# A decode step of two layers on one core: another order of the work around the two token mixers between the layers

## The chip, the cores and the metric

The kernel runs on one core of one Trainium2 chip; the other cores are idle. The time is that of one execution on the device, in microseconds (us). Three runs of the kernel before took 2510.24, 2511.62 and 2512.16 us, the median is 2511.62.

## The reference

Two layers, each an attention block and a token mixer with residuals, for B = 2 sequences with one new token each (D = 512):

```python
x = x + A(layernorm(x), k_cache, v_cache, wq, wo)   # 32 query heads, 8 K/V heads, 32768 keys, head width 128
x = x + M(layernorm(x), w1, b1, w2, b2)             # for each of the D channels: 1 token -> 1792 hidden, gelu -> 1 token
x = x + A(...)                                      # the same caches and weights again
x = x + M(...)
```

`A` is softmax attention (`q = x @ wq`, four query heads share one K/V head, scores times 128^-0.5), followed by `@ wo`. All numbers are float32. Both layers read the same caches: 2 x 8 heads x 32768 keys x 128 numbers, once for K and once for V, 537 MB in all. They don't fit on the chip, so almost all of it is read from HBM twice.

## The kernel before, in words

**Units and chunks.** A unit is one K/V head of one sequence in one layer; there are 32, numbered `n` in the order of `units`. Its K and its V are cut into 8 chunks of 4096 keys (2 MB each). `load_k` and `load_v` issue the loads, all from SyncE's (SP's) queue through `load` (L136). `k_chunk` (L413) multiplies a K chunk with the unit's query columns into a PSUM tile `scores`, one tile for chunks 0 to 3 and one for 4 to 7 (the two halves of a unit); behind the last chunk of each half a maximum is taken on VectorE (L423). `max_1` (L429 to L433) and `max_2` (L437, L439) make one maximum per head of it, `turn_scores` (L443) transposes the scores into the SBUF tiles `S[0]` and `S[1]`, and the exponential is taken by `exponentials` (L448) or, for the units 14 and 17, by `exponentials_at_once` (L460 on VectorE, L463 on ScalarE) with `sums` (L467) for the denominators. `v_chunk` (L553) multiplies the V chunks with `S` into the PSUM tile `acc`. `out_0` (L521, L523), `out_1` (L593, L595) and `out_2` (L236) bring the unit's result through `wo` into the PSUM tile `rows`.

**Memory.** The tile `mem` holds cells of 2 MB (one chunk; 16 KB per partition). Loads go to whole cells, to pairs of cells or to half cells. `spread` picks for a chunk in the middle part of the kernel: a whole cell if one is free early enough (`fit` of at least 2), otherwise two halves, each with its own load of 1 MB. A load waits until what stood in its cell has been read.

**Residents.** Of head 7 (the "keeper") the K chunks 0, 1 and 2 (cells 0, 1 and 9) and parts of V stay in the chip's memory from layer 0 to layer 1. So unit 15 (layer 1, sequence 0, head 7) starts with three K chunks that need no load, and so does unit 18 for sequence 1. Once they are read, their cells take other chunks.

**The changes of layer.** After unit N1 = 13 sequence 0 is done with the attention of layer 0, after N2 = 16 sequence 1. Then comes its mixer, while K of the next unit, which still belongs to layer 0 or to the other sequence (14, and 17), streams through. The mixer's steps: `mix_1` (L615) puts x, broadcast over the partitions, into a PSUM tile `bcast`; `take_rows` (L607, L608) copies `rows` to `S[1]`; `mix_2` adds them to `bcast` (L639) and takes mean and deviation of the layer norm (L642 to L647, one power on GpSimd, L628); `hidden_sum` makes 14 tiles, each a gelu on ScalarE (L778) and a multiply-add into `acc` on VectorE (L793, L795); `mix_3` adds the sum over partitions to `bcast` (L803), copies it out (L805) and takes the statistics of the new x (L811 to L814); `to_columns` (L302, L305, L307) turns the row into the columns of x and of its layer norm. Only then can the query of unit 15 or 18 be made (`make_q`: L338 products, L347, L351, L359).

**What sets the order.** The order is written by hand (`manual_schedule`): each engine's instructions stand in the order in which the program issues them. The main loop walks over `stream`, a list of K and V chunks sorted by a key; chunk number `t` of it is time `t`. `at(time, f, ...)` hangs a function behind that time; with half steps it stands between the two halves of a chunk. Functions of one time run by rank. The allocator (`fit`, `hold`, `booked`, `closed`) reckons in the same times. `vend` is the time at which unit n's last V chunk is done, `kend` that of its last K chunk; in a change K chunks 2 to 7 of the next unit stand at `vend` to `vend + 6`.

The order around the first change, on TensorE: V chunk 7 of unit 13; K2, first half; `out_1`; K2, second half; `out_2`; K3, first half; `mix_2`; K3, second half; K4, K5; K6, first half; `mix_3`; K6, second half; `to_columns`; K7, first half; the query products of unit 15; K7, second half; the query columns; `max_1`; resident K0 of unit 15 with `max_2` in the middle; then V and resident K in turn: V0, K1, V1, K2, V2, K3 and so on. K2 and K3 of unit 14 are loaded as whole cells, K4 to K7 and V0 to V2 as halves.

Of the kernel before, what the change touches and what calls it, by code (L numbers as in the profile page):

```python
# [13 lines left out]
P = 128  # L14
# [28 lines left out]
def gqa_mixer_kernel(ctx: ExitStack, tc: tile.TileContext, x, kt, v, wqo, cols, out):  # L43
# [118 lines left out]

    def spread(until):

        k = min((*range(WCELL0 + 1), KEPT[3][1]), key=lambda k: (-fit(k, 1, until), idle(k)))
        if fit(k, 1, until) >= 2:
            hold(k, 1, until)
            return [cells(k)]
        return [half(until - 0.5), half(until)]
# [141 lines left out]
    def unit_of(n):  # L311

        return units[n]
# [4 lines left out]
    def partner(n):  # L318

        layer, b, h = unit_of(n)  # L320
        return units.index((layer, B - 1, h)) if b == 0 and (layer == 0 or h in passing) else None

    def make_q(n, step, place=None):

# [4 lines left out]
        if n in q_kept:  # L329
            if step == 3:  # L330
                nc.vector.tensor_copy(qpad[n % 2][:, 28 : 28 + R], q_kept.pop(n))
            return
        if step == 0:

            q_ps[n] = pfix.tile([P, 512], F32, name="bcast") if N1 < n <= N3 + 2 else kept[0]
        if step < 2:
            for d in range(step * DT // 2, (step + 1) * DT // 2):
                nc.tensor.matmul(  # L338
                    q_ps[n][:m, :],
                    xnT[:, d, b : b + m],  # L340
                    wq_at(h)[:, d, :],
                    start=(d == 0),
                    stop=(d == DT - 1),
                )
        if step == 2:
# [34 lines left out]
    def load_k(n, c, m, limit):  # L380
# [4 lines left out]
        if own is not None:  # L385
            if stay and not layer:
                until = k_done[units.index((1, b, h)), c + m - 1]
            hold(own, m, until)
            bufs = [cells(own, m)]
        elif limit == RING:  # L390
            bufs = spread(until)
        else:
            bufs = [buffer(m, limit, until)]
# [9 lines left out]
    def k_chunk(n, c, part):  # L403
# [16 lines left out]
        if i == PACK - 1 and part == SUB - 1:  # L420
            if half == 0:
                mx[n] = field(n, 0, HALVES)
            nc.vector.tensor_reduce(mx[n][:, half : half + 1], sc_ps[n, half], axis=AX.X, op=ALU.max)  # L423

# [420 lines left out]
    for n in range(NU):  # L845
        stream += [(n * NCH + c + m - 1, 0, n, c, m, limit) for c, m, limit in parts(n, 0)]
        for c, m, limit in parts(n, 1):
            if n in (N1, N2):
                key = (n + 1) * NCH + 1 + (c + 1) / (2 * NCH)
            elif n in (N1 + 1, N2 + 1):  # L850
                key = (n + 1) * NCH - 0.5 + max(c / (2 * NCH) - 0.5, c + 1)
            else:
                key = (n + 1) * NCH + c + m - 1 + (LAG if N1 < n <= N3 else 0)
# [21 lines left out]
    for n in range(NU):  # L875
# [4 lines left out]
        if n:  # L880
            if n in (N1 + 2, N2 + 2):
                q0 = q1 = q2 = mixed[layer - 1, b] + 0.5
                q3 = q2 + 0.5
                place = S[1]
# [4 lines left out]
            assert q3 <= kbeg[n]  # L889
            at(q0, make_q, n, 0)  # L890
            at(q1, make_q, n, 1)
            at(q2, make_q, n, 2, place)
# [5 lines left out]
        if n in (N1 + 1, N2 + 1):  # L898
            t0 = mixed[units[n - 1][:2]]
            at(t0, turn_scores, n, 0, rank=2)  # L900
            at(kend, max_1, n)
            at(kend + 0.5, max_2, n)
            at(kend + 0.5, exponentials_at_once, n, 0)
            t1 = kend + 1
            assert t0 + 1 <= kend == kbeg[n + 1]
            at(t1, turn_scores, n, 1, rank=2)
# [29 lines left out]
        if units[n] == lay[layer, b][-1]:  # L936
            key = (layer, b)
            at(vend - 1 if change else vend, mix_1, key)
            at(vend + (1 if change else 2), take_rows, key, row_tile())
            at(vend + (1.5 if change else 3), mix_2, key)  # L940
            at(vend + (0 if change else 1), gelu_table)
            if change:

                assert k_done[n + 1, NCH - 1] == vend + 6
                at(vend + 2, hidden_sum, key, rank=2)
                at(vend + 4.5, mix_3, key)
                at(vend + 5, to_columns, key)
                mixed[key] = vend + 5
            else:
# [105 lines left out]
```

## Time and profile before

| | us |
|---|---|
| median of three runs | 2511.62 |
| the profiled execution, its own time | 2510.26 |
| its span (first to last instruction) | 2508.5 |
| TensorE matmuls, busy | 1386.6 (55%) |
| TensorE weight loads, busy | 372.2 (15%) |
| VectorE, busy | 239.9 (10%) |
| ScalarE, busy | 188.0 (7%) |
| HBM, read | 1063.81 MB, 424 GB/s over the span |
| loads of the caches and weights, share of 16 DMA engines | 98.8% |

The busy digits of the page cut the span into 40 slices of 62.7 us. The mean granted clock of TensorE is 0.767. In the rows of groups the columns are: line, engine, operation, output and inputs, count, then busy us, mean ns of one, and the idle time before them with what ended it. A matmul of the program is two on the engine here (float32), so eight records make the four matmuls of one half chunk.

### The profile page before, as it was taken

The numbers are of one execution on the slowest core, as the hardware profiler recorded it, in microseconds if no ns is written. First come the engines' busy times: TensorE is split into PE (matmuls) and PEld (weight loads), VectorE is DVE, ScalarE is ACT, GpSimd is POOL, SyncE is SP. The second block draws the span as 40 slices with busy tenths as digits, with TensorE's granted clock in tenths as the row PEclk, the third lists the DMA queues.
The fourth block names the chain that finished last, engine by engine and source line by source line (L and its number), as shares of the span: only waits on it lengthen the run. The fifth ranks groups of instructions, "written<-read, shape, count | busy, mean of one in ns | idle before, by whom it ended". The sixth has DMA issues, their size and how long they took to land.

```text
span 2508.5 us, 20487 instructions
## 1 busy us (share of the span) xinstructions
PE 1386.6 (55%) x9270; PEld 372.2 (15%) x9270; DVE 239.9 (10%) x632; ACT 188.0 (7%) x554; POOL 4.9 (0%) x17
## 2 busy tenths in 40 slices
PE   4555554645445554666577676355546555455556
PEld 1111111111111111111121121111111111111112
DVE  0000000000000000004013110000000000010002
ACT  0000000000000000002012010000000000012002
POOL 0000000000000000000000000000000000000000
PEclk8777777777777777888797887777777777777778
DMA  9999999999999999999999999999999999999996
GB/s 419 433 433 433 434 434 431 432 429 434 432 433 432 433 429 432 430 426 381 426 426 404 395 428 433 433 433 432 430 432 431 432 429 430 434 432 435 433 431 285
DMA packets 33504, 1065.14 MB, mean 425 GB/s; under 512 B 3973, under 2 KB 3977, under 8 KB 4874
## 3 DMA queue, kind: packets, MB, share of 16 engines
q1 hardware_dynamic: 33128, 1063.80, 98.8%
q8 instruction: 73, 1.20, 0.2%
q14 instruction: 13, 0.11, 0.0%
q10 hardware_dynamic: 290, 0.04, 0.0%
HBM read 1063.81 MB, written 0.00 MB: 424 GB/s over the span
## 4 chain that ended last, share of the span: by engine, by line
DMA 73%; PE 24%; DVE 1%; issue 1%; ACT 0%; SPq 0%; POOL 0%; DVEq 0%; ACTq 0%
DMA mem<-in_v_dram 37%; DMA mem<-in_kt_dram 36%; PE scores L413 11%; PE acc L553 10%; PE kept L338 1%; DVE acc L795 1%; PE rows L236 0%; PE bcast L338 0%; PE small L437 0%; PE small L593 0%; PE bcast L803 0%; PE small L584 0%; PE kept L735 0%; PE small L351 0%; PE small L302 0%
## 5 line engine op out<-in xcount | busy, mean ns | idle before, releaser
L413 PE MATMUL scores<-mem,small_sb 128*32 128x512 f32 x4096 | 635.3, 737 | 612.5 <-DMA mem<-in_kt_dram 612.4
L553 PE MATMUL acc<-mem,S 128*16 128x512 f32 x4088 | 614.1, 740 | 456.6 <-DMA mem<-in_v_dram 455.1
L413 PEld LDWEIGHTS scores<-mem,small_sb 128*32 128x32 f32 x4096 | 149.0, 128 | 997.6 <-issue 892.0
L448 ACT ACTIVATE S<-S,small_sb 128x128 f32<-128x128 f32 x240 | 123.6, 519 | 2112.4 <-DVE small_sb L439 1640.2
L553 PEld LDWEIGHTS acc<-mem,S 128*16 128x16 f32 x4088 | 134.1, 111 | 832.7 <-issue 687.9
L423 DVE TENSOR_REDUCE small_sb<-scores 128x1 f32<-128x512 f32 x64 | 44.2, 691 | 914.6 <-PE scores L413 914.6
L443 DVE STREAM_TRANSPOSE S<-scores 128x512 f32<-128x512 f32 x64 | 45.5, 710 | 129.9 <-PE acc L553 129.9
L338 PE MATMUL kept<-mem,small_sb 128*2 128x512 f32 x104 | 51.0, 616 | 1.7 <-DVE small_sb L264 1.7
L236 PE MATMUL rows<-mem,small_sb 128*1 128x512 f32 (+1 forms) x276 | 47.7, 604 | 2.6 <-ACT mem L778 2.4
L448 ACT ACTIVATION_READ_ACCUMULATOR S<-S,small_sb 128x1 f32 x240 | 44.9, 187 | 0.0
L433 DVE TENSOR_REDUCE small_sb<-small 1x4 f32<-1x128 f32 x32 | 8.9, 279 | 278.0 <-PE small L431 278.0
L523 DVE SCALAR_TENSOR_TENSOR S<-acc,small_sb,S 128x128 f32<-128x128 f32 x93 | 32.6, 351 | 3.3
L595 DVE TENSOR_TENSOR small_sb<-small,small_sb 128x4 f32<-128x4 f32 x31 | 5.1, 164 | 290.8 <-PE small L593 290.8
L586 DVE RECIPROCAL small_sb<-small 128x4 f32<-128x4 f32 x32 | 5.9, 184 | 280.6 <-PE small L584 280.6
L778 ACT ACTIVATE S<-bcast,small_sb 128x512 f32<-128x512 f32 x28 | 21.5, 777 | 98.9 <-DVE small_sb L647 96.8
L351 PE MATMUL small<-small_sb,mem 2*128 2x2 f32 x112 | 15.1, 253 | 17.9 <-DVE mem L347 17.9
L521 DVE TENSOR_SCALAR S<-acc,small_sb 128x128 f32<-128x128 f32 x31 | 10.8, 349 | 112.6 <-PE acc L553 112.6
L338 PE MATMUL bcast<-mem,small_sb 128*1 128x512 f32 (+1 forms) x40 | 19.4, 617 | 0.0
L593 PEld LDWEIGHTS small<-small_sb,S 128*128 128x128 f32 x62 | 12.4, 249 | 44.9 <-issue 40.6
L351 PEld LDWEIGHTS small<-small_sb,mem 2*128 2x128 f32 x112 | 14.0, 191 | 30.5 <-DVE mem L347 27.3
L795 DVE SCALAR_TENSOR_TENSOR acc<-S,small_sb,acc 128x512 f32<-128x512 f32 x24 | 18.1, 755 | 2.5
L431 PE MATMUL small<-small_sb 128*1 128x128 f32 x64 | 16.1, 343 | 0.6 <-DVE small_sb L429 0.6
(134 smaller groups left out, 268.1 us busy)
## 6 DMA issues: line engine op xcount, KB each, us to landing
mem<-in_kt_dram SPq DMA_DIRECT2D x35, 2048.0 KB, 20.7
mem<-in_v_dram SPq DMA_DIRECT2D x26, 2048.0 KB, 21.7
mem<-in_v_dram SPq DMA_DIRECT2D x9, 4096.0 KB, 30.0
mem<-in_wqo_dram SPq DMA_DIRECT2D x14, 2048.0 KB, 33.7
mem<-in_kt_dram SPq DMA_DIRECT2D x7, 4096.0 KB, 27.4
mem<-in_kt_dram SPq DMA_DIRECT2D x18, 1024.0 KB, 9.2
mem<-in_v_dram SPq DMA_DIRECT2D x17, 1024.0 KB, 10.4
mem<-in_v_dram SPq DMA_DIRECT2D x2, 1280.0 KB, 27.2
```

Source lines behind the costliest of these rows:

```text
L236: nc.tensor.matmul(rows[32 * g : 32 * g + b + 1, :], weights if b else weights[:, 1:], row, start=False, stop=True, skip_group_check=True,)
L338: nc.tensor.matmul(q_ps[n][:m, :], xnT[:, d, b : b + m], wq_at(h)[:, d, :], start=(d == 0), stop=(d == DT - 1),)
L351: nc.tensor.matmul(pt[:, r * m : (r + 1) * m], q_row[n][:m, r * DH : (r + 1) * DH], ident[:m, :m], start=True, stop=True,)
L413: nc.tensor.matmul(sc_ps[n, half][32 * g : 32 * g + 32, :], q, kc[k * NG + g], start=(i == 0 and k == 0), stop=(i == PACK - 1 and k == SUB ...
L423: nc.vector.tensor_reduce(mx[n][:, half : half + 1], sc_ps[n, half], axis=AX.X, op=ALU.max)
L431: nc.tensor.matmul(pm[:1, :P], mxa, ident, start=True, stop=True)
L443: nc.vector.transpose(S[half], sc_ps[n, half])
L448: nc.scalar.activation(s[:, :, h], s[:, :, h], AF.Exp, bias=neg[n][:, h : h + 1], scale=SCALE, accum_out=lsum[n][:, half, h : h + 1],)
L523: nc.vector.scalar_tensor_tensor(t, acc[:, k * DH : (k + 1) * DH], mask[:, k : k + 1], t, op0=ALU.mult, op1=ALU.add)
L553: nc.tensor.matmul(acc[32 * g : 32 * g + R * QT, :], S[half][:, col : col + R * QT], vc[q], start=(c == 0 and q < NG), stop=(c == NCH - 1 ...
L778: nc.scalar.activation(hid[key, f], px[key], AF.Gelu_apprx_tanh, bias=shift[key][:, f : f + 1], scale=slope[key][:, f : f + 1],)
L795: nc.vector.scalar_tensor_tensor(h if f == FT - 1 else acc, h, w, acc, op0=ALU.mult, op1=ALU.add)
```

## The change

Around each of the two changes of layer, and nowhere else:

- `mix_2` stands right behind `out_2` and `take_rows`, ahead of K3, and `hidden_sum` right behind it, ahead of K3's instructions instead of behind them.
- `mix_3` stands behind the second half of K6 instead of between its halves, `to_columns` and `turn_scores` of the first half between the halves of K7.
- The maximum of the first half of unit 14 (and 17) is taken behind K6's first half, so behind `hidden_sum` on VectorE.
- The query products of unit 15 (and 18) stand behind K7 and are cut up: one ahead of `max_1`, one ahead of `max_2`, two behind the exponential of the first half. The columns of the query follow V0.
- V0 and V1 of unit 14 (and 17) stand ahead of the resident K0, and each later V chunk of that unit two K chunks earlier than before, so that the order is V0, V1, K0, V2, K1, V3, K2, V4, K3 and so on; at its end K6 and K7 of unit 15 (and 18) follow each other with no V between. The second half's scores are turned behind V1.
- K2 and K3 of unit 14 (and 17) are loaded as halves. What follows from that and from the new order: V3 and V4 of unit 14 are loaded as halves too, and V2 and V3 of unit 17. There are 8 loads more in all, of the same bytes.

```diff
-    def spread(until):
+    def spread(until, parted=False):
...
-        if fit(k, 1, until) >= 2:
+        if fit(k, 1, until) >= 2 and not parted:
...
+    def q_products(n, *ds):
+
+        layer, b, h = unit_of(n)
+        m = 1 if partner(n) is None else B
+        for d in ds:
+            if d == 0:
+                q_ps[n] = pfix.tile([P, 512], F32, name="bcast") if N1 < n <= N3 + 2 else kept[0]
+            nc.tensor.matmul(
+                q_ps[n][:m, :],
+                xnT[:, d, b : b + m],
+                wq_at(h)[:, d, :],
+                start=(d == 0),
+                stop=(d == DT - 1),
+            )
...
         if step < 2:
-            for d in range(step * DT // 2, (step + 1) * DT // 2):
...
+            q_products(n, 2 * step, 2 * step + 1)
...
-            bufs = spread(until)
+            bufs = spread(until, n in (N1 + 1, N2 + 1) and c > 1)
...
-            nc.vector.tensor_reduce(mx[n][:, half : half + 1], sc_ps[n, half], axis=AX.X, op=ALU.max)
+            if half or n not in (N1 + 1, N2 + 1):
+                highest(n, half)
+
+    def highest(n, half):
+
+        nc.vector.tensor_reduce(mx[n][:, half : half + 1], sc_ps[n, half], axis=AX.X, op=ALU.max)
...
             elif n in (N1 + 1, N2 + 1):
-                key = (n + 1) * NCH - 0.5 + max(c / (2 * NCH) - 0.5, c + 1)
+                key = (n + 1) * NCH - 0.5 + max(c / (2 * NCH) - 0.5, c - 1)
...
             if n in (N1 + 2, N2 + 2):
-                q0 = q1 = q2 = mixed[layer - 1, b] + 0.5
-                q3 = q2 + 0.5
+                q2 = mixed[layer - 1, b]
+                q3 = q2 + 1
...
-            at(q0, make_q, n, 0)
-            at(q1, make_q, n, 1)
+            if n not in (N1 + 2, N2 + 2):
+                at(q0, make_q, n, 0)
+                at(q1, make_q, n, 1)
...
         if n in (N1 + 1, N2 + 1):
-            t0 = mixed[units[n - 1][:2]]
-            at(t0, turn_scores, n, 0, rank=2)
+            at(kend - 0.5, turn_scores, n, 0, rank=2)
+            at(kend, q_products, n + 1, 0)
             at(kend, max_1, n)
-            at(kend + 0.5, max_2, n)
-            at(kend + 0.5, exponentials_at_once, n, 0)
-            t1 = kend + 1
-            assert t0 + 1 <= kend == kbeg[n + 1]
+            at(kend, q_products, n + 1, 1)
+            at(kend, max_2, n)
+            at(kend, exponentials_at_once, n, 0)
+            at(kend, q_products, n + 1, 2, 3)
+            t1 = kend + 2
+            assert mixed[units[n - 1][:2]] == kend == kbeg[n + 1] - 2
...
-            at(vend + (1.5 if change else 3), mix_2, key)
+            at(vend + (1 if change else 3), mix_2, key)
...
-                at(vend + 2, hidden_sum, key, rank=2)
-                at(vend + 4.5, mix_3, key)
-                at(vend + 5, to_columns, key)
-                mixed[key] = vend + 5
+                at(vend + 1, hidden_sum, key)
+                at(vend + 4.5, highest, n + 1, 0)
+                at(vend + 5, mix_3, key)
+                at(vend + 5.5, to_columns, key)
+                mixed[key] = vend + 6
```

More of the change, by code (lines that the diff above doesn't have):

```diff
@@ L332, in make_q @@
             return
-        if step == 0:
-            q_ps[n] = pfix.tile([P, 512], F32, name="bcast") if N1 < n <= N3 + 2 else kept[0]
         if step < 2:
-            for d in range(step * DT // 2, (step + 1) * DT // 2):
[L338 to L344, printed above, removed]
+            q_products(n, 2 * step, 2 * step + 1)
         if step == 2:
```

## The prediction, made before the changed kernel ran

> **What bounds the kernel now.** I read the page first: busy tenths by slice, then the chain that ended last.
>
> ```profile
> span 2508.5 us, 20487 instructions
> DMA  9999999999999999999999999999999999999996
> GB/s 419 433 433 433 434 434 431 432 429 434 432 433 432 433 429 432 430 426 381 426 426 404 395 428 433 433 433 432 430 432 431 432 429 430 434 432 435 433 431 285
> DMA 73%; PE 24%; DVE 1%; issue 1%; ACT 0%; SPq 0%; POOL 0%; DVEq 0%; ACTq 0%
> ```
>
> The transfers are the bound: the DMA row is 9 almost to the end and they fill 73% of the chain. But the GB/s row sags in the slices with 381, 404 and 395, and there lie the two places that the change touches: the token mixer of batch 0 (after unit 13) and that of batch 1 (after unit 16), both of layer 0. I cut both out with the view by windows; its last two columns are the DMA share and GB/s.
>
> ```profile
> 1150.00:1174.00 24.00, 14.57 (x84) 2.48 (x76) 14.77 (x25) 12.86 (x17) 0.54 (x1) 0.80 1.00 407
> 1174.00:1194.00 20.00, 19.03 (x146) 6.36 (x142) 7.94 (x18) 1.26 (x2) 0.54 (x1) 0.99 0.86 306
> 1194.00:1214.00 20.00, 10.16 (x64) 2.05 (x64) 1.46 (x3) 0.00 (x0) 0.00 (x0) 0.83 1.01 430
> 1340.00:1370.00 30.00, 19.59 (x110) 3.65 (x102) 16.28 (x29) 12.85 (x17) 0.54 (x1) 0.76 1.00 420
> 1370.00:1386.00 16.00, 15.03 (x84) 5.48 (x84) 6.99 (x17) 1.26 (x2) 0.54 (x1) 0.82 0.60 212
> 1386.00:1406.00 20.00, 15.34 (x114) 4.33 (x106) 2.83 (x7) 0.00 (x0) 0.00 (x0) 1.00 1.01 431
> ```
>
> Against the 430 of the undisturbed rows, 20 us at 306 lose 20 x (1 - 306/430) = 5.77 us and 16 us at 212 lose 8.11: 13.88 us in which the DMA engines had nothing to do. The rows at 407 and 420 lose 1.28 and 0.70 more. Since the rest of the span is a stream at full rate, every us of this that goes is a us off the end.
>
> **Why it runs dry.** In a mixer the loads have five half cells of 1 MB (K chunks 2.5, 7, 7.5, 8, 8.5 in turn). A half is reloaded when TensorE has read it, so a wait on TensorE becomes a late load. First mixer, timeline (start, us, engine, line; in brackets the idle time before and what ended it):
>
> ```profile
> 1143.42 3.38 PE L553 MATMUL acc<-mem,S 128*16 128x512 f32 x16 [1.90 <-DMA mem<-in_v_dram]
> 1147.23 1.12 DVE L523 SCALAR_TENSOR_TENSOR S<-acc,small_sb,S 128x128 f32<-128x128 f32 x3
> 1148.31 1.07 PE L413 MATMUL scores<-mem,small_sb 128*32 128x512 f32 x8 [1.51 <-DMA mem<-in_kt_dram]
> 1149.31 0.39 PE L593 MATMUL small<-small_sb,S 128*128 128x4 f32 x2
> 1151.61 0.69 DVE L607 COPY S<-rows 128x512 f32<-128x512 f32 x1 [1.72 <-PE rows L236]
> 1153.21 1.06 PE L413 MATMUL scores<-mem,small_sb 128*32 128x512 f32 x8 [1.66 <-DMA mem<-in_kt_dram]
> 1154.20 1.12 PE L639 MATMUL bcast<-S,small_sb 128*128 128x512 f32 x2
> 1157.75 1.45 ACT L778 ACTIVATE S<-bcast,small_sb 128x512 f32<-128x512 f32 x2 [49.99 <-DVE small_sb L647]
> 1158.16 1.06 PE L413 MATMUL scores<-mem,small_sb 128*32 128x512 f32 x8 [0.98 <-DMA mem<-in_kt_dram]
> 1165.64 1.06 PE L413 MATMUL scores<-mem,small_sb 128*32 128x512 f32 x8 [0.94 <-DMA mem<-in_kt_dram]
> 1169.72 0.75 DVE L795 SCALAR_TENSOR_TENSOR S<-S,small_sb,acc 128x512 f32<-128x512 f32 x1
> 1170.53 2.08 PE L803 MATMUL bcast<-S,small_sb 128*128 128x512 f32 x2 [3.82 <-DVE S L795]
> 1176.27 3.17 PE L338 MATMUL bcast<-mem,small_sb 128*1 128x512 f32 x7
> 1180.81 0.69 DVE L423 TENSOR_REDUCE small_sb<-scores 128x1 f32<-128x512 f32 x1 [0.23 <-PE scores L413]
> 1185.20 1.91 PE L553 MATMUL acc<-mem,S 128*16 128x512 f32 x16 [0.65 <-ACT S L463]
> ```
>
> K chunk 6a (the first half) is read at 1165.64. TensorE then stands before L803 until the hidden sum ends at 1170.47, and afterwards has the query products (L338) and the maxima before the first V chunk, 1185.20. The loads behind these waits, from the timeline of SP and from the DMA issues of those windows (last column: us to landing):
>
> ```profile
> 1174.53 0.33 SPq L136 DMA_DIRECT2D mem<-in_v_dram  x1
> 1180.80 0.33 SPq L136 DMA_DIRECT2D mem<-in_v_dram  x1
> 1186.32 0.33 SPq L136 DMA_DIRECT2D mem<-in_v_dram  x1
> 1383.26 0.33 SPq L136 DMA_DIRECT2D mem<-in_v_dram  x1
> ```
>
> ```profile
> mem<-in_kt_dram SPq DMA_DIRECT2D x7, 1024.0 KB, 9.5
> mem<-in_v_dram SPq DMA_DIRECT2D x4, 1024.0 KB, 6.9
> mem<-in_v_dram SPq DMA_DIRECT2D x2, 1024.0 KB, 5.8
> ```
>
> The first is 1149 to 1165, the second 1174 to 1187, the third 1370 to 1384. A half takes 1.05 MB / 430 = 2.4 us to move, so a load must be issued 6.9 - 2.4 = 4.5 us (second mixer 3.4) before the queue runs dry. V1a (1174.53) just held; V2a (1180.80) and V2b (1186.32) came too late, and so did V2 of the second mixer (1383.26, a whole cell).
>
> **Part 1: halves for K2 and K3, statistics right behind the output rows.** Half of K2 lands 2.4 us ahead of the whole, at 1145.9, so K2a runs when V7 ends (1143.42 + 3.38 = 1146.8); L593 then waits only for DVE (1147.23 + 1.12 = 1148.35) and starts at 1148.4, 0.9 us earlier than 1149.31. The copy of the rows ends at 1151.61 + 0.69 - 0.9 = 1151.4, and L639, no longer behind K3a, starts there and not at 1154.20: 2.8 us earlier. So does all that hangs on it: gelus from 1154.95, hidden sum done at 1167.7. K3a waits 1.1 us behind L639, with its load's room not needed for 7 us: nothing. Second mixer:
>
> ```profile
> 1344.40 1.30 PE L413 MATMUL scores<-mem,small_sb 128*32 128x512 f32 x8 [2.99 <-DMA mem<-in_kt_dram]
> 1350.30 1.12 PE L639 MATMUL bcast<-S,small_sb 128*128 128x512 f32 x2
> 1361.73 1.93 PE L413 MATMUL scores<-mem,small_sb 128*32 128x512 f32 x8 [0.55 <-DMA mem<-in_kt_dram]
> 1365.82 0.75 DVE L795 SCALAR_TENSOR_TENSOR S<-S,small_sb,acc 128x512 f32<-128x512 f32 x1
> 1366.62 2.08 PE L803 MATMUL bcast<-S,small_sb 128*128 128x512 f32 x2 [2.96 <-DVE S L795]
> 1383.85 1.91 PE L553 MATMUL acc<-mem,S 128*16 128x512 f32 x16 [0.65 <-ACT S L463]
> ```
>
> There K2a moves from 1344.40 to 1341.9. From the start of L593 to the end of the copy it took 3.0 us in the first mixer; from the landing of K2b (1344.4) that gives 1347.4 for L639 instead of 1350.30: sum done at 1363.7 instead of 1365.82 + 0.75 = 1366.57.
>
> **Part 2: the sum (L803) behind K6b.** With a queue that never empties halves land every 2.48 us (1165.64 - 1158.16 over the three halves between these two reads, each released by a DMA). So K6b lands at 1168.1, after the sum is ready (1167.7). TensorE waits for data alone: K6b ends at 1169.2, L803 at 1170.3 (1.12 us as L639) to 1171.3 (2.08 as now), K7a (landed 1170.6), the columns, K7b (1173.0) ends at 1174.1 to 1175.2. Its loads follow: V1a at 1169.3 (now 1174.5), V2a at about 1174.7 (now 1180.80). All have over 7 us of queue ahead. The maximum of the first half (0.69 us of DVE) moves behind the sum into the 2.8 us in which DVE waits for L803: nothing, and 0.7 us ahead of V0 if that wait were gone. POOL has only the two powers of the statistics, which move with them.
>
> **Part 3: queries in the wait for maxima, V0 and V1 ahead of the resident K0.** Seven of the eight passes of the four products take 3.17 us, so one product 0.9. In the kernel before they stand ahead of K7b's maximum; now one stands before each of the two small matmuls of the maxima and two beside the exponential. From the maximum to V0 it took 1185.20 - 1180.81 = 4.4 us; with up to 0.6 more for products in front I take 4.7 to 5.5 from K7b's end: V0 at 1178.9 to 1180.7. V0a frees the room of V2b, issued at 1180.0 to 1181.8. The queue then holds V0b, V1a, V1b, V2a and ends at 1185.4: lead 3.6 to 5.4 against the 4.5 needed, a loss of 0 to 0.9, taken as 0.3. In the second mixer the same steps give V2b at 1376.2 to 1378.0 against a queue end of 1361.73 + 8 x 2.48 = 1381.5: also 0.3 at most. Behind it V3a, V3b, V4a, V4b follow TensorE with leads of 6 us and more (V0b 1181.3, then 1.1 us of query columns, V1, then K0 1.9 us, V2a 1186.3). On SP the load into K0's room now stands behind four halves of V; it is issued at 1188 with 7 us in the queue: nothing. Resident K0 no longer covers V0's wait; the price of that is rival 4.
>
> **Part 4: more halves.** In each mixer four chunks of 2 MB more are loaded as halves (K2, K3 and V3, V4; second V2, V3): 16.8 MB at 420 GB/s (window 1340:1370, almost all halves) instead of 430 costs 0.93 us, and 6.3 MB that now run in the dry stretches 0.35. The Trainium skill, "DMA: Bandwidth & Descriptors", section "Bandwidth", speaks against such a cut: it measured 341 GB/s for 1 MB against 425 for 16 MB. That is one transfer by itself, and the row of 420 disagrees for halves in a full queue; by the page the 16.8 MB would cost 10.2 us, and the whole come to some 2508 (an estimate).
>
> **Sum.** 13.88 - 0.6 - 1.28 = 12.0 us. The profiled execution took 2510.26 (span 2508.5), so 2498.3; the three runs' median is 1.4 higher, so 2499.6 against it. I say **2499.0**.
>
> **Rivals.** (1) The chain from the hidden sum, not the data, still sets V0: it now takes 1185.20 - 1170.47 = 14.7 and 1383.85 - 1366.57 = 17.3 us. Kept whole, V0 comes at 1182.4 and 1381.0, V2b 1.1 later, and 2.6 and 4.0 us stay lost: 13.88 - 6.6 - 1.3 = 6.0, **2504.3**. Against it: in these chains lie K6b, K7b and all query products, which now stand elsewhere. (2) TensorE runs at the lower clock through V and resident K, which alternate there: K 3.6 us a chunk instead of 1.9.
>
> ```profile
> 1198.22 2.74 PE L413 MATMUL scores<-mem,small_sb 128*32 128x512 f32 x12 [3.80 <-DMA mem<-in_kt_dram]
> ```
>
> That is 12 of 16 matmuls, so 3.6 the chunk. V0 then ends at 1182.8, V1 with the query columns at 1187.4, K0 at 1191.0, V2a at 1192.8. V4b, issued then, has a queue to 1185.4 + 4 x 2.48 = 1195.3, a lead of 2.5 against 4.5: 2 us in each mixer, 12.0 - 4.0 = 8.0, **2502.3**. Against it: 0.99 granted in 1174:1194, where TensorE is busy throughout. "TensorE: Matmul & The Clock Gate" of the Trainium skill, section "Part 1", has the lower clock after some 3.4 us idle; the trace agrees for L803 (3.82 idle, 2.08 us), and the wait before V0 is near that. (3) Halves fall to the 306 GB/s of the dry row: the extra 16.8 MB cost 54.9 - 39.1 = 15.8 us, 13.88 - 0.6 - 0.35 - 15.8 = -2.9, **2513**. Against it: 420. The rule of the Trainium skill in part 4 points this way. (4) Slower: TensorE's queue is in order, so V0's wait for the exponential now holds all resident chunks too, whose rooms used to come free beside it. From a wait of 11.5 us after K7b (V2b at 1186.7, 1186.7 + 4.5 - 1185.4 = 5.8 lost) the first mixer gains nothing, and each us more costs one. If the 14.7 of rival 1 stood behind K7b, 9.0 and 8.0 would be lost, 3.1 more than now, and with 1.3 for the halves it is **2515**. Against it: 4.4 measured.
>
> **Chances.** Forecast 0.68, rivals 0.13, 0.09, 0.04, 0.06. The range goes from 2495 (all of 13.88 and most of the 2 us of the 407 and 420 rows gone) to 2505, which takes in rivals 1 and 2. Faster by over 0.2% (5 us, about what a measurement of this kernel can tell from no change): 0.68 + 0.13 + 0.09 = 0.90, within 0.04, slower 0.06.
>
> **What would show it.** In the new profile slices 19 to 23 of the GB/s row should read about 420 to 430. L639 should start right behind the copy of the rows; L803 should no longer be released by DVE but follow K6b; V0 should start some 5 us after K7b's maximum; V2b should be issued before its queue ends. Wrong would be: a DMA share below 0.9 in the 20 us behind K7b, or a rate under 410 with a full queue.

## The result and the profile after

The changed kernel takes **2499.86 us** (median of 6 runs, 2499.0 to 2501.82); the kernel before, run beside it on the same chip, 2510.14 us (6 runs, 2507.17 to 2512.16). The ratio is 0.9961, 95% interval 0.9948 to 0.9974: some 10 us faster. The forecast was 2499.0 in a range of 2495 to 2505. The profiled execution took 2499.0 us with a span of 2497.2, so 11.3 us of span went. From the page of the kernel after, GB/s by slice and chain:

```profile
GB/s 420 435 435 425 437 432 433 432 431 434 435 433 430 431 432 433 428 426 411 427 426 421 428 420 427 435 434 433 429 431 436 433 429 432 436 431 432 431 431 288
DMA 74%; PE 25%; issue 0%; DVE 0%; ACT 0%; SPq 0%; POOL 0%; DVEq 0%
```

The transfers are still the bound. The slices that read 381, 404 and 395 now read 411, 421 and 428. The same six stretches in the view by windows (last three columns: granted TensorE clock, DMA share, GB/s):

```profile
1150.00:1174.00 24.00, 15.98 (x100) 3.37 (x93) 16.10 (x29) 12.86 (x17) 1.09 (x2) 0.85 1.01 409
1174.00:1194.00 20.00, 17.61 (x110) 4.93 (x106) 6.67 (x14) 1.26 (x2) 0.00 (x0) 0.84 0.99 403
1194.00:1214.00 20.00, 11.39 (x84) 2.11 (x76) 1.36 (x3) 0.00 (x0) 0.00 (x0) 0.91 1.01 430
1340.00:1370.00 30.00, 21.62 (x120) 4.63 (x120) 18.21 (x34) 13.15 (x18) 1.08 (x2) 0.89 1.01 421
1370.00:1386.00 16.00, 12.97 (x109) 3.71 (x108) 4.57 (x8) 0.97 (x2) 0.00 (x0) 1.00 1.02 424
1386.00:1406.00 20.00, 14.40 (x99) 3.89 (x94) 2.15 (x4) 0.00 (x0) 0.00 (x0) 0.91 1.01 428
```

The two dry windows went from 306 to 403 and from 212 to 424. Against 430 they now lose 20 x (1 - 403/430) = 1.26 and 16 x (1 - 424/430) = 0.22 us, where they lost 5.77 and 8.11: 12.4 us won. By the same reckoning 1.35 us are given back far away, at 1460 to 1480 (last section). The first mixer's timeline:

```profile
1147.25 0.39 PE L603 MATMUL small<-small_sb,S 128*128 128x4 f32 x2
1148.57 1.06 PE L418 MATMUL scores<-mem,small_sb 128*32 128x512 f32 x8 [0.93 <-DMA mem<-in_kt_dram]
1150.56 0.69 DVE L617 COPY S<-rows 128x512 f32<-128x512 f32 x1 [2.72 <-PE rows L236]
1151.31 1.12 PE L649 MATMUL bcast<-S,small_sb 128*128 128x512 f32 x2 [0.81 <-DVE S L617]
1154.85 1.45 ACT L788 ACTIVATE S<-bcast,small_sb 128x512 f32<-128x512 f32 x2 [47.77 <-DVE small_sb L657]
1158.50 1.07 PE L418 MATMUL scores<-mem,small_sb 128*32 128x512 f32 x8 [1.34 <-DMA mem<-in_kt_dram]
1160.97 1.94 PE L418 MATMUL scores<-mem,small_sb 128*32 128x512 f32 x8 [1.41 <-DMA mem<-in_kt_dram]
1166.82 0.75 DVE L805 SCALAR_TENSOR_TENSOR S<-S,small_sb,acc 128x512 f32<-128x512 f32 x1
1168.43 1.07 PE L418 MATMUL scores<-mem,small_sb 128*32 128x512 f32 x8 [0.95 <-DMA mem<-in_kt_dram]
1169.43 1.12 PE L813 MATMUL bcast<-S,small_sb 128*128 128x512 f32 x2
1180.03 1.91 PE L563 MATMUL acc<-mem,S 128*16 128x512 f32 x16
1181.14 3.14 SPq L136 DMA_DIRECT2D mem<-in_v_dram  x3
1189.73 1.05 PE L563 MATMUL acc<-mem,S 128*16 128x512 f32 x8 [2.39 <-DMA mem<-in_v_dram]
```

The lines have moved by ten: L649 is the product of the statistics, L805 the last step of the hidden sum, L813 the sum over partitions, L563 the V products. L813 has no bracket: it follows K6b at once, for 1.12 us where L803 took 2.08. The last two rows are V2b's load (the first of the three in its row, issued at 1181.14) and the product that waits for it. The second mixer:

```profile
1361.80 1.12 PE L813 MATMUL bcast<-S,small_sb 128*128 128x512 f32 x2
1370.39 1.91 PE L563 MATMUL acc<-mem,S 128*16 128x512 f32 x16
```

### The profile page after: what moved, and what is told of

The parts are those of the page before. It is cut to its first block, busy times and chain, and to the rows that moved or that the text cites. A ratio compares the mean times of both kernels' runs of the same rounds, so it can differ in the third digit from the quotient of the medians.

```text
span 2497.2 us, 20499 instructions
## 1 busy us (share of the span) xinstructions
PE 1385.6 (55%) x9270; PEld 371.4 (15%) x9270; DVE 240.3 (10%) x632; ACT 187.8 (8%) x554; POOL 4.9 (0%) x17
## 4 chain that ended last, share of the span: by engine, by line
DMA 74%; PE 25%; issue 0%; DVE 0%; ACT 0%; SPq 0%; POOL 0%; DVEq 0%
DMA mem<-in_v_dram 38%; DMA mem<-in_kt_dram 37%; PE scores L418 11%; PE acc L563 10%; PE kept L330 1%; PE bcast L330 1%; PE rows L236 0%; PE small L447 0%; PE small L603 0%; PE small L594 0%; PE kept L745 0%; PE small L441 0%; SPq L136 0%; ACT S L458 0%; PE small L356 0%
## 5 line engine op out<-in xcount | busy, mean ns | idle before, releaser
L563 PE MATMUL acc<-mem,S 128*16 128x512 f32 x4088 | 618.4, 743 | 462.1 <-DMA mem<-in_v_dram 457.2
L563 PEld LDWEIGHTS acc<-mem,S 128*16 128x16 f32 x4088 | 135.3, 111 | 833.1 <-issue 683.4
L236 PE MATMUL rows<-mem,small_sb 128*1 128x512 f32 (+1 forms) x276 | 49.8, 635 | 2.6 <-ACT mem L788 2.3
L805 DVE SCALAR_TENSOR_TENSOR acc<-S,small_sb,acc 128x512 f32<-128x512 f32 x24 | 18.1, 754 | 2.5
L603 PEld LDWEIGHTS small<-small_sb,S 128*128 128x128 f32 x62 | 11.5, 232 | 45.0 <-issue 37.9
L441 PE MATMUL small<-small_sb 128*1 128x128 f32 x64 | 17.3, 365 | 0.2 <-DVE small_sb L439 0.2
## 6 DMA issues: line engine op xcount, KB each, us to landing
mem<-in_kt_dram SPq DMA_DIRECT2D x26, 1024.0 KB, 11.3
```

Source lines behind the costliest of these rows:

```text
L236: nc.tensor.matmul(rows[32 * g : 32 * g + b + 1, :], weights if b else weights[:, 1:], row, start=False, stop=True, skip_group_check=True,)
L441: nc.tensor.matmul(pm[:1, :P], mxa, ident, start=True, stop=True)
L563: nc.tensor.matmul(acc[32 * g : 32 * g + R * QT, :], S[half][:, col : col + R * QT], vc[q], start=(c == 0 and q < NG), stop=(c == NCH - 1 ...
L805: nc.vector.scalar_tensor_tensor(h if f == FT - 1 else acc, h, w, acc, op0=ALU.mult, op1=ALU.add)
```

## Experiments

The theory on trial, the **lead theory**: the queue runs dry because V0, and with it the loads that wait for its room, is late; the reordering brings V0 forward, by its earlier start and by its order in about equal parts. Its rivals are named in each expectation. Below, "V0 at +x / +y" is the start of the first V product, counted from the second record of the product of `out_1` (L593, in the changed kernel L603), first / second mixer: before +35.8 / +38.0, changed kernel +32.7 / +31.4. The product of `out_1` itself moves (first mixer: 1149.31 before, 1147.25 changed), so where that matters the start in the first mixer is given too: 1185.20 before, 1180.03 changed. Rows and windows are those of one profiled execution, which can lie some us off the median. Each median stands beside those of the kernel before from the same call: 2509.4 for the first four runs, 2510.3 for the next four, 2511.3 for the three of the clock, 2510.8 for the last.

### The early start alone

The kernel before with K2 and K3 in halves and the statistics and hidden sum behind the output rows; the sum, the queries and V as before.

```diff
+            bufs = spread(until, n in (N1 + 1, N2 + 1) and c > 1)
...
+            at(vend + (1 if change else 3), mix_2, key)
...
+                at(vend + 1, hidden_sum, key)
```

> The kernel before with the earlier start of the mixer alone (K2 and K3 in halves, statistics right behind the output rows); sum, query products and the order of V and resident K stay. Lead theory (time is lost only where the load into V2b's room is issued less than 4.5 to 6 us before the queue of loads ends): first gelu 2.8 us earlier in both mixers, V0 at about 1182.4 and 1381, about half of the gain: 2504 to 2506 us. Rival (the earlier start is the whole gain): 2500 us.

**2500.2 us** (2499.48 to 2501.22; ratio 0.9963, 0.995 to 0.9976): the rival's number, the whole measured gain. Its second mixer on TensorE:

```profile
1359.34 1.48 PE L413 MATMUL scores<-mem,small_sb 128*32 128x512 f32 x8 [0.56 <-DMA mem<-in_kt_dram]
1360.99 1.12 PE L803 MATMUL bcast<-S,small_sb 128*128 128x512 f32 x2 [0.17 <-DVE S L795]
1363.05 1.05 PE L302 MATMUL small<-small_sb,S 128*128 128x1 f32 x8
1365.19 3.17 PE L338 MATMUL bcast<-mem,small_sb 128*1 128x512 f32 x7
1374.13 1.91 PE L553 MATMUL acc<-mem,S 128*16 128x512 f32 x16 [0.65 <-ACT S L463]
```

The kernel before has these in the same place, in the same order. Here are K5b, which lies well ahead of its L803 (2.08 us), and behind L803 K6b, the columns and, behind K7a, the products:

```profile
1359.24 1.93 PE L413 MATMUL scores<-mem,small_sb 128*32 128x512 f32 x8 [1.43 <-DMA mem<-in_kt_dram]
1368.62 1.94 PE L413 MATMUL scores<-mem,small_sb 128*32 128x512 f32 x8
1370.49 1.87 PE L302 MATMUL small<-small_sb,S 128*128 128x1 f32 x8
1374.00 4.08 PE L338 MATMUL bcast<-mem,small_sb 128*1 128x512 f32 x7
```

The columns (L302) take 1.05 us here in place of 1.87, the query products (L338) 3.17 in place of 4.08. From the hidden sum's end to V0 it is 13.2 us in place of 17.3. TensorE stood 0.17 us ahead of L803 in place of 2.96. So the chain of the second mixer got shorter with its order untouched, and a new theory arose, the **clock theory**: it is not the wait for the sum that costs most but the low clock that TensorE has behind it. In the kernel before the low clock did not begin with that wait: K5b already took 1.93 us, and the granted clock of the whole stretch from 1359 to 1374 is 0.50. The wait at most kept it low.

In the first mixer the start did less: V0 at 1183.73 is 1.5 us earlier than before, L803 took 2.08 us here too, behind a wait of only 1.35, and the window reads 354 GB/s in place of 306. In the second mixer it reads 410 in place of 212.

### Parts of the order alone, or taken back

V0 and V1 ahead of the resident K0 in the kernel before, nothing else:

```diff
+                key = (n + 1) * NCH - 0.5 + max(c / (2 * NCH) - 0.5, c - 1)
...
+            at(kend, max_2, n)
+            at(kend, exponentials_at_once, n, 0)
+            t1 = kend + 2
```

> The kernel before with V0 and V1 ahead of the resident K0 alone. Lead theory: V0 still waits for a hidden sum that ends at 1170.5 and for the query products ahead of K7b, so it starts at about 1184.5 instead of 1185.2 and V2b's load at about 1185.6: 0 to 2 us gained, 2508 to 2510 us. Rival (the order of V and resident K is the gain): 2500 to 2503 us.

2509.57 us (2504.69 to 2513.32; 0.9991 to 1.001): no difference. In the first mixer V0 stayed where it was (1185.10, +35.1), with 320 GB/s in the window. In the second it came at +35.0, 3.0 us earlier, with 310 GB/s in place of 212; but that profiled execution took 2506.69, and the median of the ten shows nothing of it.

The changed kernel with K0 ahead of V0 again:

```diff
-                key = (n + 1) * NCH - 0.5 + max(c / (2 * NCH) - 0.5, c - 1)
+                key = (n + 1) * NCH - 0.5 + max(c / (2 * NCH) - 0.5, c + 1)
...
-                q3 = q2 + 1
+                q3 = q2
```

> The changed kernel with the resident K0 ahead of V0 again, as before. K0 needs the query's columns, which now come behind the exponential, so V0 should start 5 us later than in the changed kernel, V2b's load at about 1186 and 1376.5. Lead theory: 5 to 6 us more lost in the first mixer, 2 to 5 in the second: 2507 to 2510 us. Rival (the earlier start is the whole gain): 2500 us.

2502.15 us (0.9966 to 0.9985), between the two expectations: V0 at +37.0 / +35.4 (1184.34 in the first mixer). So a V0 that starts 4.3 and 4.0 us later than in the changed kernel cost 2.3 us here, far less than the lead theory had.

The changed kernel with all four query products ahead of K7b:

```diff
-            at(kend, q_products, n + 1, 0)
...
-            at(kend, q_products, n + 1, 1)
...
-            at(kend, q_products, n + 1, 2, 3)
+            at(kend - 0.5, q_products, n + 1, 0, 1, 2, 3, rank=3)
```

> The changed kernel with all four query products ahead of the second half of K7, as before. Lead theory: the second half of K7 comes 3 to 3.6 us later, V0 about 2.5 us later; 2.5 us more lost in the first mixer, 0 to 2 in the second: 2502 to 2505 us. Rivals: the place of the products costs nothing, 2500 us; or all of the wait returns, 2507 us.

2504.24 us (0.9973 to 0.9992), the time that the lead theory had: V0 at +32.9 / +36.2. In the first mixer `out_1` came late too, so the +32.9 hides that V0 started at 1182.03, 2.0 us later than in the changed kernel; in the second it was 4.8 later, more than forecast. With the sum behind K6b the products ahead of K7b are in the way.

The changed kernel with the products behind V0's first half and the query columns behind V1:

```diff
-            at(kend, q_products, n + 1, 0)
...
-            at(kend, q_products, n + 1, 1)
...
-            at(kend, q_products, n + 1, 2, 3)
+            at(kend + 0.5, q_products, n + 1, 0, 1, 2, 3)
```

> The changed kernel with all four query products between the halves of V0 and the query's columns behind V1. Lead theory: V0 starts 0.8 to 1 us earlier, V2b's load with it, the first mixer loses up to 1 us less, the second nothing less (its lead of 6.0 us was enough): 2498.5 to 2500 us. Rival (resident K0, which then waits for the query behind V1, delays V2): 2 to 4 us lost, 2502 to 2504 us.

2500.7 us (0.9948 to 0.9977), not told apart from the changed kernel, though V0 in the first mixer started at 1178.22, 1.8 us earlier (+29.8 / +31.0; `out_1` came 1.0 later). A V0 earlier than the changed kernel's bought nothing measurable. By itself this run could hide a gain, because K0 now waits for columns behind V1; the last run below, which leaves them in place, says the same.

The changed kernel with K2 and K3 whole:

```diff
-            bufs = spread(until, n in (N1 + 1, N2 + 1) and c > 1)
+            bufs = spread(until)
```

> The changed kernel with K2 and K3 as whole cells again (4 loads fewer). Lead theory: the mixer starts 0.9 us later in the first and about 2.5 us later in the second change, but its sum still ends about when K6b lands, so V0 hardly moves; 0 to 0.5 us less for fewer halves: 2499 to 2500.5 us. Rival (every us of the earlier start counts): 3.4 us lost, 2503 us.

2498.72 us (0.9939 to 0.9972), the fastest median but not to be told from 2499.86: once the rest stands, these halves bring nothing and cost at most about 1 us. The run shows more than that. In its first mixer the statistics start no earlier than in the kernel before (L649 at 1154.14, there L639 at 1154.20), and the hidden sum ends at 1170.42, there at 1170.47. Yet V0 starts at 1179.89, 5.3 us earlier:

```profile
1170.47 2.07 PE L813 MATMUL bcast<-S,small_sb 128*128 128x512 f32 x2
1179.89 1.91 PE L563 MATMUL acc<-mem,S 128*16 128x512 f32 x16
```

From the sum's end to V0 it is 9.5 us in place of 14.7, with L813 at the low clock as before. Nor is there an early start in the second mixer: L649 comes 6.8 us after K2 has landed, L639 before 5.9. So the new order brings the whole gain without the early start, just as the early start brought it without the new order.

### V0 later by a known amount

Copies of `S[0]` onto itself on ScalarE ahead of the exponential of units 14 and 17, 7 and 13 of them; nothing is left out.

```diff
+        for _ in range(7 if half == 0 else 0):
+            nc.scalar.activation(S[half], S[half], AF.Copy)
         nc.scalar.activation(S[half], S[half], AF.Exp)
```

> The changed kernel with seven copies of the first half's scores onto themselves (ScalarE) ahead of its exponential in the units 14 and 17, about 4.3 us in front of V0. Lead theory: V2b's lead falls from 4.6 to about 0.3 in the first mixer (4 us more lost) and from 6.0 to 1.7 in the second (1.7 to 4.3 lost): 2505.5 to 2508.5 us. Rivals: no slack at all, 2508.6 us; a delay of V0 hidden by the queue, 2500 us.

> The same with thirteen copies, about 8 us in front of V0, so some 12.5 to 13 us from the second half of K7 to V0: the point from which the slower rival of the prediction decides (11.5 us). Lead theory: 8 us more lost in the first mixer, 5.4 to 8 in the second: 2513 to 2516 us, slower than the kernel before (2510). Rival (hidden by the queue): 2500 us.

2507.31 us (0.9978 to 0.9997) and **2513.59 us** (1.0006 to 1.0025, slower than before). V0 came at +36.7 / +36.0 and +40.0 / +40.0: 4.1 and 4.6, then 7.4 and 8.6 us later than in the changed kernel. The medians rose by 7.5 and 13.7 us for 8.7 and 15.9 us of delay, 0.86 us a microsecond. The two windows of the 13 copies (the dry stretch reaches beyond the second, with 351 GB/s in 1386 to 1406):

```profile
1174.00:1194.00 20.00, 11.41 (x68) 3.10 (x64) 5.50 (x11) 9.44 (x15) 0.00 (x0) 0.83 0.64 259
1370.00:1386.00 16.00, 7.00 (x36) 2.24 (x36) 4.67 (x12) 8.81 (x14) 0.54 (x1) 0.85 0.78 324
```

So in this order a late V0 is dear, as both theories have it. But the price is not that of V0's start alone: with K0 ahead of V0 (above) V0 stood as late as with the seven copies, 1184.34 against 1184.43 in the first mixer, and that cost 2.3 us, not 7.5. The copies hold back all that stands behind V0 on TensorE, the resident chunks too: the next load of K is issued at 1186.63 there and at 1195.99 with the seven copies. That is the mechanism of the fourth rival; that it makes the whole difference of the two runs is argued, not shown.

### The clock alone

The kernel before with nothing moved; products of the 128x128 unit matrix with itself (`idle_products`, which the kernel already has for its last mixer) keep TensorE busy while the hidden sum runs. Nobody uses them.

```diff
+                at(vend + 3, idle_products, 4, rank=3)
+                at(vend + 3.5, idle_products, 4, rank=3)
+                at(vend + 4, idle_products, 4, rank=3)
+                at(vend + 4.5, idle_products, 8, rank=0)
                 at(vend + 4.5, mix_3, key)
```

> The kernel before with nothing moved; in the two changes' mixers four products of the 128x128 unit matrix with itself (0.29 us each at the full clock, by the eight passes in 1.16 us that line 615 takes) behind each of three K halves during the hidden sum, and eight of them (2.3 us, and twice that at the low clock) in TensorE's queue right ahead of the sum of the mixer. They leave nothing out and compute nothing that is used. What they do is keep TensorE from idling 3.82 and 2.96 us ahead of the sum. Clock theory (the start-only run gained at the second mixer because TensorE no longer idled ahead of the sum): the sum's product takes 1.1 in place of 2.08 us, and the time from the hidden sum's end to V0 falls from 14.7 and 17.3 us to 13 to 14 us, so V0 comes 1 and 3.5 us earlier, at a microsecond each: 2504.5 to 2507. Rival (that chain is set by VectorE, ScalarE and the loads, or the start alone made the difference): 2509.5 to 2511.

**2503.15 us** (2500.99 to 2505.13; 0.9972, 0.996 to 0.9983), 8.2 us less than 2511.31, without moving one instruction of the kernel. First mixer on TensorE, then the two windows:

```profile
1165.78 1.07 PE L413 MATMUL scores<-mem,small_sb 128*32 128x512 f32 x8 [0.33 <-DMA mem<-in_kt_dram]
1166.77 2.05 PE L683 MATMUL small<-small_sb 128*128 128x128 f32 x16
1170.63 1.12 PE L803 MATMUL bcast<-S,small_sb 128*128 128x512 f32 x2 [1.80 <-DVE S L795]
```

```profile
1174.00:1194.00 20.00, 17.80 (x134) 5.18 (x126) 7.43 (x15) 1.26 (x2) 0.15 (x1) 1.00 0.93 370
1370.00:1386.00 16.00, 15.04 (x123) 4.83 (x116) 6.54 (x13) 1.26 (x2) 0.00 (x0) 1.00 0.86 351
```

L683 are the added products; L803 still waits for the sum (1.80) and takes 1.12 us. From the sum's end to V0 it is 13.0 us in both mixers, where it was 14.7 and 17.3; V0 at +34.0 / +33.9. The windows lose 20 x (1 - 370/430) + 16 x (1 - 351/430) = 5.7 us in place of 13.9, 8.2 less; the medians differ by 8.2 too, the two profiled executions by 9.3. The clock theory holds: the clock alone, without order or start, is worth most of the gain. The time is better than the expected 2504.5 to 2507, and the 8.2 are more than the 5.8 us that V0 came earlier in both mixers together, so V0 alone does not account for it. K7b is read earlier as well (V2a's load at 1179.1, before 1180.80). The run does not tell the products behind the three K halves from the eight ahead of the sum.

The early start without the halves:

```diff
+            at(vend + (1 if change else 3), mix_2, key)
...
+                at(vend + 1, hidden_sum, key)
```

> The kernel before with the statistics and the hidden sum put right behind the output rows, and K2 and K3 loaded whole as before: the start-only run without its halves. Lead theory with the halves a small thing (forecast 0.93 + 0.35 us for them): rows, statistics and V0 about 1 us later than in the start-only run at each mixer, 2500.5 to 2503. Rival (the early start needs the halves, since the statistics come behind whole K2 in TensorE's queue): 2505 to 2508.

2510.16 us (2500.64 to 2511.79 in 11 runs; 0.998 to 1.0001): not told apart from before, and slower even than the rival's 2505 to 2508. Two of the eleven executions took 2500.64 and 2501.26, though, as the early start with halves did; the profiled one took 2510.32, and what those two did otherwise is not known. In the first mixer the statistics came as early as planned and V0 later than before, at +36.6 (second mixer +37.8):

```profile
1152.31 1.12 PE L639 MATMUL bcast<-S,small_sb 128*128 128x512 f32 x2 [0.81 <-DVE S L607]
1168.63 2.08 PE L803 MATMUL bcast<-S,small_sb 128*128 128x512 f32 x2 [1.09 <-DVE S L795]
1172.51 1.87 PE L302 MATMUL small<-small_sb,S 128*128 128x1 f32 x8
1176.02 4.15 PE L338 MATMUL bcast<-mem,small_sb 128*1 128x512 f32 x7
1185.94 1.91 PE L553 MATMUL acc<-mem,S 128*16 128x512 f32 x16 [0.65 <-ACT S L463]
```

L639 starts 1.9 us earlier than in the kernel before (1154.20) and L803 as much (1170.53); the low clock then eats it all between L803 and V0. An early start is worth nothing if TensorE spends it at the low clock. In the second mixer there was no early start to spend: L639 came at 1350.19, before at 1350.30.

The same with added products:

```diff
+            at(vend + (1 if change else 3), mix_2, key)
...
+                at(vend + 1, hidden_sum, key)
+                for half_chunk in (3, 3.5, 4, 4.5):
+                    at(vend + half_chunk, idle_products, 4, rank=0)
```

> The statistics-only run (before with statistics and hidden sum right behind the output rows, K2 and K3 whole) with four products of the unit matrix with itself (1.16 us at the full clock) behind each of four K halves during the hidden sum; they compute nothing that is used. In the statistics-only run the first mixer's hidden sum ended 1.9 us earlier after the first V load's output product, but V0 0.8 us later, because TensorE ran the stretch from the fourth K chunk to the query products at the low clock. Clock theory: at the full clock V0 comes 13 us behind the sum's end, 32.2 and 33.4 us behind that product, in place of 36.6 and 37.8: 3.5 to 4.4 us earlier at each mixer, 2499.5 to 2502.5. Rival (the start needs the halves of K2 and K3 for something else than the clock): 2503 and over, no better than the kernel before with the added products alone.

2503.7 us (0.9961 to 0.9984): the rival's number, no better than the added products alone. The reason is the clock again, at a place that I had not covered. The second mixer:

```profile
1341.78 1.93 PE L413 MATMUL scores<-mem,small_sb 128*32 128x512 f32 x8 [2.99 <-DMA mem<-in_kt_dram]
1345.87 1.93 PE L236 MATMUL rows<-mem,small_sb 128*2 128x512 f32 x8
1348.62 1.13 PE L639 MATMUL bcast<-S,small_sb 128*128 128x512 f32 x2 [0.81 <-DVE S L607]
1364.95 1.96 PE L803 MATMUL bcast<-S,small_sb 128*128 128x512 f32 x2 [3.68 <-DVE S L795]
```

TensorE waits 2.99 us for whole K2, and K2 and the output rows (L236) behind it run at the low clock, 1.93 us for the rows where the changed kernel takes 1.04: the statistics start late after all. And four products were too few ahead of the sum: 3.68 us of idling, and L803 at 1.96. The first mixers of four runs part the clock from the halves. With K2 whole, L639 starts at 1152.31 where the rows take 1.04 us (the run before this one) and at 1153.89 where they take 1.96 (this run). With halves its counterpart starts at 1151.31 with the rows at 1.04 (the changed kernel) and at 1153.09 with the rows at 1.82 (the early start alone). So the clock is worth 1.6 to 1.8 us at this place and the halves 0.8 to 1.0, and halves by themselves don't keep the clock high.

The changed kernel with such products:

```diff
+                for half_chunk in (2.5, 3, 3.5, 4, 4.5):
+                    at(vend + half_chunk, idle_products, 4, rank=0)
                 at(vend + 5, mix_3, key)
```

> The changed kernel, with four products of the unit matrix with itself (1.16 us at the full clock, into the idle stretches of 1.3 to 1.5 us) behind each of five K halves while the hidden sum runs; they compute nothing that is used. Clock theory with the lead theory: the first mixer's query products come back from 1.91 and 1.16 us a pair to 1.02, V0 1 to 1.5 us earlier, V2b issued 5.6 to 6.1 us ahead of the queue's end in place of 4.6, and the 1.4 us that it lost is won: 2498 to 2499.5. Rival (the stretch is set by the loads of K7b and by VectorE): 2499.9 as the changed kernel. Slower, 2501 and over, if the added products hold up the K halves.

2499.06 us (2498.4 to 2499.96; 0.994 to 0.9967): inside the first expectation, but not to be told from 2499.86. V0 came earlier in the first mixer, at 1178.68 (+29.9 / +31.4), and V2b's load too, the first of the two issued at 1179.79:

```profile
1178.68 1.91 PE L563 MATMUL acc<-mem,S 128*16 128x512 f32 x16
1179.79 1.19 SPq L136 DMA_DIRECT2D mem<-in_v_dram  x2
1184.79 1.91 PE L563 MATMUL acc<-mem,S 128*16 128x512 f32 x8 [2.23 <-DMA mem<-in_v_dram]
```

That is 1.35 us earlier, yet V2b landed at 1189.71, where it did at 1189.68 in the changed kernel: this time V1b, issued at 1172.06, was late (1184.79). So the last 1.4 us of the first mixer are not won by lead alone. What holds them stays open.

## Why the prediction was right, and where its reasons were not

**What bounds it, and the price of a dry queue:** right. 12.4 of the 13.88 us of the two windows went, and delaying V0 in the changed kernel cost 0.86 us a microsecond.

**Part 1, first mixer:** right to 0.2 us in its times: L649 at 1151.31 (1151.4 forecast), gelus at 1154.85 (1154.95), sum done at 1166.82 + 0.75 = 1167.57 (1167.7). Its path was another, and that the times fit is partly luck: L603 started at 1147.25, 1.1 us ahead of the forecast 1148.4, and then the rows had to wait for K2b (1148.57, released by its load), which the forecast had not put between. Second mixer: sum done at 1359.29, 7.3 us earlier than before; the first mixer's window had gained 4.5 by then, and 2.8 of its own is what 1366.57 to 1363.7 said.

**Part 2:** right: L813 behind K6b at 1169.43 (1169.2), ending at 1170.55, the early end of its range. V1a was issued at 1169.56 (1169.3) and V2a at 1175.07 (1174.7).

**Part 3:** V0 at 1180.03 and V2b at 1181.14 lie inside 1178.9 to 1180.7 and 1180.0 to 1181.8. The loss of 0.3 was too small: V2b landed at 1189.68, 1.4 us later than a full queue would have brought it (V1b landed at 1183.2, and two more halves of 2.48 us make 1188.2), and the window still loses 1.26. In the second mixer V0 started at 1370.39, 13.5 us earlier, 9 of its own, with no loss at V2b (0.22 in the window).

**Part 4:** the rate of halves was right (421 and 424 against 420 assumed). The price of 1.28 us for all of them is not contradicted: K2 and K3 whole gave 1.1 us less, inside the noise. The estimate by the Trainium skill ("DMA: Bandwidth & Descriptors", section "Bandwidth", 341 GB/s for 1 MB) came to 2508; the windows at 421 and 424 and the 2499.86 us disagree with it for halves in a full queue.

**The step that failed** is the adding up of the two moves. Rival 1 has the early start with the chain behind it kept whole, which leaves 2.6 and 4.0 us lost and comes to 2504.3; the start alone was expected from it. As a run it gave 2500.2, and its windows lost 3.5 and 0.7 us: the second mixer makes the difference. Two things were missing.

First, rival 1 kept the chain from the hidden sum to V0 at 14.7 and 17.3 us, as if its length were a matter of order alone, and rival 2 looked for the low clock only behind V0. The runs show that some 4 of the second mixer's 17.3 us were the clock. With the order of before, 17.3 became 13.2 by the early start and 13.0 by the added products; between L803 and L338 the rows give 2.08 - 1.12 = 0.96, K6b 1.94 - 1.07, the columns 1.87 - 1.05, K7a 1.93 - 1.06 and the products 4.08 - 3.17: 4.4 us in all (the K7a rows, 1.93 and 1.06, are not shown). The row that says so (L803: 3.82 us of idling, then 2.08) stood in the prediction.

Second, the gains do not add. Order shortens the chain too, as the prediction held against rival 1: with the sum ending as before, 14.7 became 9.5 in the run with K2 and K3 whole, and that run took 2498.72. The start alone gave 2500.2, the clock alone 2503.15, and neither the order on top of the start, nor the start on top of the order, nor products on top of the change is worth a measurable microsecond. So the forecast of the sum came out although its shares did not: it took nearly the whole loss as won, and either move wins nearly the whole.

**The clock.** "TensorE: Matmul & The Clock Gate" of the Trainium skill, section "Part 1", has the low clock after an idle window of about 3.4 us and the full clock after as long a busy one. The waits of 3.82 and 3.68 us with 2.08 and 1.96 us behind them agree, and so do 1.80 with 1.12. But L803 also took 2.08 us behind waits of 2.96, 1.35 and 1.09, each time behind a K half that had already run at 1.93 or 1.94. And the trace shows the low clock set in without such a wait: in the changed kernel K halves of 1.06 us with waits of about 1.4 between them drop to 1.94 at 1160.97, where the longest wait of the stretch is 1.50. With products in the gaps (0.33 us left) they stay at 1.07.

## What to carry to other kernels

Where a chain of small TensorE steps stands on the critical path, compare the duration of one step there with the same step elsewhere (here 2.08 against 1.12, 1.87 against 1.05) before reordering anything: a few unused products in the idle time ahead of it may win most of what a new order would. Count a wait ahead of such a chain twice, once as the wait and once as the low clock that it leaves behind or keeps up. And when several moves go in together and the sum comes out, run each alone all the same: here the start alone had the whole gain, the order without the early start had it too, V ahead of K0 alone had none, and the total told nothing of any of them.

## What the runs showed of the hardware beside that

The changed kernel loses 20 x (1 - 401/430) = 1.35 us at 1460 to 1480, long after the mixers, and the variant with K2 and K3 whole does not, though the loads and products there are of the same order. The window of the changed kernel and the V product in it:

```profile
1460.00:1480.00 20.00, 14.46 (x94) 3.49 (x95) 2.31 (x4) 0.00 (x0) 0.00 (x0) 0.74 1.00 401
```

```profile
1462.45 1.91 PE L563 MATMUL acc<-mem,S 128*16 128x512 f32 x8 [4.59 <-DMA mem<-in_v_dram]
```

And of the variant:

```profile
1460.00:1480.00 20.00, 14.10 (x95) 3.49 (x96) 2.57 (x4) 0.00 (x0) 0.00 (x0) 0.83 1.02 429
```

```profile
1462.10 1.19 PE L563 MATMUL acc<-mem,S 128*16 128x512 f32 x8 [4.28 <-DMA mem<-in_v_dram]
```

After almost the same wait the product ran at the low clock in one (1.91) and mostly at the full clock in the other (1.19). That the clock makes the loss is only argued, and two things speak against it: the loads there were issued 8 us and more ahead of their landing, and in the run with K0 ahead of V0 the product ran at 1.91 too (at 1466.24, behind a wait of 3.21), while the stretch from 1455 to 1480 held 423 GB/s. A second thing that no run tested: one 16 KB packet of instructions holds a DMA engine for about 1.1 us, by the row of the run with products in the changed kernel, a window of 14 us (0.5% of 16 engines):

```profile
q8 instruction: 1, 0.02, 0.5%
```

It lies at 1182.5, between V1b's issue and its late landing. In the changed kernel one lies between 1186 and 1187, between V2b's issue and its landing. Whether they cause the lateness is open; there are 73 of them in each execution, so one can easily lie there by chance.
